# The gate of a fused attention and feed-forward kernel as one over one plus an exponential

## The chip, the cores and the metric

The kernel runs on one core of one Trainium2 chip. The metric is the time of one execution on the device in microseconds (us). Over three runs the kernel before the change took 1265.78, 1266.6 and 1267.1 us; the median is 1266.6 us.

The engines are named as the profile names them. PE is the matrix engine, and PEld its loading of weights. DVE is the vector engine, ACT the scalar engine (activation functions and copies), POOL the third elementwise engine, and SP the queue that issues the DMAs. Each engine works through its own instructions in order and waits on semaphores for the others.

## What is computed

The first half is attention of 512 local and 32 global tokens for 8 batches and 8 heads of width 64. Its output is the input `x` of a gated feed-forward layer of 4608 tokens, 512 channels and 1536 hidden channels. The change touches only the gate:

```python
def _moe_ref(x, w_gate, w_val, w_out) -> np.ndarray:
    gate = 1.0 / (1.0 + np.exp(-(x @ w_gate)))
    val = x @ w_val
    return (gate * val @ w_out).astype(np.float32)
```

## The kernel before

Matmuls run on float32r operands. Each operand is split into a high and a low part, and three of the four products are summed, so a product of two matrices costs three matmuls per block. The high part is a copy on ACT, the low part a subtraction on POOL.

`ffn_stream` walks through 120 **items**. An item is one chunk of tokens with one of the 12 blocks of 128 hidden channels. The first 24 items belong to two half chunks of 256 tokens and alternate between them; the next 84 belong to seven chunks of 512 tokens; the last 12 to one chunk of 256 global tokens. For an item PE issues 12 matmuls into a PSUM bank `bank_g` (the gate), 12 into `bank_v` (the value), and then the matmuls into `bank_o` that belong to the item before it. Between `bank_g` and `bank_o` the other engines do the following (tile names in the profile's manner):

- ACT L370: `th` = tanh of half of `bank_g`
- DVE L375: `mn` = the smaller of `bank_g` and 0, then ACT L376: `mn` = its exponential. For every second of the first 24 items ACT L372 and L373 do this in place of DVE and ACT.
- ACT L377: `th` = its absolute value
- DVE L378: `th` = (`th` + 1) times `mn`, which is twice the gate
- DVE L380: `th` = `bank_v` times `th`
- ACT L382 and POOL L383: the high and low parts `hh`, which are the operand of the `bank_o` matmuls

The factor 2 is taken out when the finished `bank_o` is copied to `ob` (L402 on ACT, L404 on DVE).

Attention of the next chunk runs between the groups of these matmuls, and so up to the last chunk but one of 512 tokens. Its units (two blocks of 128 queries of a head, or the global queries of a head) are generators with four stages that a queue of events starts at fixed ticks of the feed-forward. A unit's way over the engines is: scores on PE (L225), masked and reduced on DVE (L237), exponential on ACT (L240), reciprocal of the row sums on DVE (L243, L244), normalising mostly on DVE (L213, `p_buf`), transposition on PE (L254), high part on ACT (L263) and low part on DVE (L264, `pt`), product with the values on PE (L280, L281), and the sum of its parts (ACT L283, DVE L284, POOL L285). The global unit has the same steps in L299 to L337. The first chunks' attention runs without the splits, and the first 24 items also share DVE, ACT and POOL with the conversion of the weights (L128 to L138).

The python order of these calls is the starting point; a scheduler then arranges the instructions of each engine, so the order on an engine isn't the order of the lines. `bank_g`, `bank_v` and the attention's `bank_x` and `bank_y` share four PSUM banks in turn (tag "att"), and a bank is free again only when DVE or ACT has read it. `th` and `mn` have one buffer each.

Of the kernel before, what the change touches and what calls it, by code (L numbers as in the profile page):

```python
# [8 lines left out]
F32 = mybir.dt.float32  # L9
F32R = mybir.dt.float32r  # L10
U32 = mybir.dt.uint32
AF = mybir.ActivationFunctionType
ALU = mybir.AluOpType
# [4 lines left out]
P = 128  # L18
# [11 lines left out]
WIN = 224  # L30
DM = 512

# Where work is issued, in ticks of the feed-forward (one tick is four 512-token
# matmuls). Attention units of a chunk follow each other every PER ticks; a unit's
# stages lie STAGES apart, its operands are loaded and split ahead of it.
BASE, PER = 3, 4
STAGES = (0, 3, 6, 9)
LOAD_QK, LOAD_V, SPLIT_QK, SPLIT_V = 16, 9, 10, 4
LOAD_V_NATIVE = 4
# from the first of these ticks of a chunk on, attention is put off by the second  # L40
HOLE = (8, 1)
START = dict(per0=4, base1=1, per1=1.1, base2=23, per2=3, x2=28, lead=8, native_heads=4)
CONVERT = (-2, 4, 1, 3)
CONVERT_EARLY = (-985, -980, -977)
# the engines that share a kind of operation in turn: v(ector), s(calar)
NORM = {0: "v", 1: "v", 2: "ssv", 3: "sv"}
REBASE = "vs"

# [1 line left out]
NF = DF // P  # L50
KT = DM // P
# [3 lines left out]
def kernel(ctx, tc, qk, v, w_gate, w_val, w_out, out_l, out_g):  # L55
    nc = tc.nc
# [10 lines left out]
    ffn = ctx.enter_context(tc.tile_pool(name="ffn", bufs=1))  # L67
    dram = ctx.enter_context(tc.tile_pool(name="dram", bufs=1, space=DRAM))
    ps = ctx.enter_context(tc.tile_pool(name="ps", bufs=1, space=PSUM))

# [1 line left out]
    ident = const.tile([P, P], F32, name="ident")  # L72
    make_identity(nc, ident)
    NEG = -8.0e9
    masks = const.tile([P, 3, WIN], F32, name="masks")
    nc.gpsimd.memset(masks[:, 1], 0.0)
    # window column c < 96 stands for key c - 32, c >= 128 for key c - 64
    # (relative to the block's first query); the columns between are global
    mid = masks[:, 1]
    for c0, lo, hi in ((0, 0, 64), (128, 96, -32)):  # L80
        cols = mid[:, c0:c0 + 96]
# [13 lines left out]
    nc.vector.memset(pg, 0.0)  # L95
    xg32 = const.tile([P, KT, NG], F32, name="xg32")

# [1 line left out]
    wg = [const.tile([P, KT, DF], F32R, name=f"wg{i}") for i in range(2)]  # L99
    wv = [const.tile([P, KT, DF], F32R, name=f"wv{i}") for i in range(2)]  # L100
    wo_dram = [dram.tile([P, 2, DM], F32, name=f"wo_dram{f}") for f in range(NF)]
# [15 lines left out]
            nc.sync.dma_start(st, src)  # L117

    def convert(i, hi, lo):
        """The two float32r parts of a float64 [128, KT or 1, n] block, given as words."""  # L120
        src = w_src[i]
        t, n = src.shape[1], src.shape[2] // 2
        st, v = (o[i % len(o)].rearrange("p (t n) -> p t n", t=t) for o in conv_bufs)
        words = st.rearrange("p t (n two) -> p t n two", two=2)
        low, high = words[:, :, :, 0], words[:, :, :, 1]
        vf, hf = v.bitcast(F32), high.bitcast(F32)
        with tc.issue_after(anchor[0].ins) if i < 3 else nullcontext():
            nc.vector.tensor_scalar(v, high, 0x80000000, None, op0=ALU.bitwise_and)  # L128
            # read as a float32, the high word times 2^-112 has its exponent rebased to
            # float32's, with zeros between the sign and the exponent's eight bits  # L130
            if REBASE[i % len(REBASE)] == "s":
                nc.scalar.mul(hf, hf, 2.0 ** -112)
            else:
                nc.vector.tensor_scalar(hf, hf, 2.0 ** -112, None, op0=ALU.mult)
            nc.vector.scalar_tensor_tensor(v, low, 29, v, op0=ALU.logical_shift_right, op1=ALU.bitwise_or)
            nc.vector.scalar_tensor_tensor(v, high, 3, v, op0=ALU.logical_shift_left, op1=ALU.bitwise_or)
        nc.scalar.copy(hi, vf)
        nc.gpsimd.tensor_tensor(lo, vf, hi.bitcast(F32), op=ALU.subtract)  # L138
        stage(i + len(conv_bufs[0]))
# [9 lines left out]
        nc.sync.dma_start(wo_dram[f][:, 0], hi[:, 0].bitcast(F32))  # L149
        nc.sync.dma_start(wo_dram[f][:, 1], lo[:, 0].bitcast(F32))  # L150

# [1 line left out]
    def qcol(j):  # L153
        return j * P if j < 2 else Q1 + (j - 2) * P

# [180 lines left out]
        nc.vector.tensor_tensor(y, o_ps[0:64], y, op=ALU.add)  # L336
        nc.gpsimd.tensor_tensor(xg, y[:, 0:32], y[:, 32:64], op=ALU.add)  # L337

# [1 line left out]
    hl_q = []  # L340

    def x_split(xt, x32, kt, x0, ntok):
# [2 lines left out]
        nc.gpsimd.tensor_tensor(xt[:, 1, kt, xs], x32[:, 0:ntok], xt[:, 0, kt, xs].bitcast(F32), op=ALU.subtract)  # L345

    def ffn_stream(items):
        """Items (chunk, block of the hidden dimension); yields the part of a full
        512-token step that was issued, between groups of matmuls."""
        prev = None  # L350
        wo = None
        for n_it in range(len(items) + 1):
            if n_it < len(items):
                C, f = items[n_it]
                ntok, x0, xt = C["ntok"], C["x0"], C["xt"]()
                fs = slice(f * P, (f + 1) * P)
                for w, nm in ((wg, "bank_g"), (wv, "bank_v")):
                    acc = ps.tile([P, 512], F32, name=nm, tag="att", bufs=4)[:, 0:ntok]
                    n = 0
                    for a, c in ((0, 0), (1, 0), (0, 1)):  # L360
                        for t in range(KT):
                            nc.tensor.matmul(acc, w[a][:, t, fs], xt[:, c, t, x0:x0 + ntok],  # L362
                                             start=n == 0, stop=n == 11)
                            n += 1
                        if n < 12:
                            yield ntok / 512
                    if nm == "bank_g":
                        th = ffn.tile([P, 512], F32, name="th", bufs=1)[:, 0:ntok]
                        mn = ffn.tile([P, 512], F32, name="mn", bufs=1)[:, 0:ntok]
                        nc.scalar.activation(th, acc, AF.Tanh, scale=0.5)  # L370
                        if n_it < 2 * NF and n_it % 2:
                            nc.scalar.activation(mn, acc, AF.Relu, scale=-1.0)  # L372
                            nc.scalar.activation(mn, mn, AF.Exp, scale=-1.0)  # L373
                        else:
                            nc.vector.tensor_scalar(mn, acc, 0.0, None, op0=ALU.min)  # L375
                            nc.scalar.activation(mn, mn, AF.Exp)  # L376
                        nc.scalar.activation(th, th, AF.Abs)  # L377
                        nc.vector.scalar_tensor_tensor(th, th, 1.0, mn, op0=ALU.add, op1=ALU.mult)  # L378
                    else:
                        nc.vector.tensor_tensor(th, acc, th, op=ALU.mult)  # L380
                        hh = ffn.tile([P, 2, 512], F32R, name="hh", bufs=2)
                        nc.scalar.copy(hh[:, 0, 0:ntok], th)  # L382
                        nc.gpsimd.tensor_tensor(hh[:, 1, 0:ntok], th, hh[:, 0, 0:ntok].bitcast(F32), op=ALU.subtract)  # L383
                    yield ntok / 512
                if not (wo is not None and items[n_it - 1][1] == f):
                    wo = ffn.tile([P, 2, DM], F32R, name="wo", bufs=2)
                    nc.sync.dma_start(wo.bitcast(F32), wo_dram[f])
            if prev is not None:
                C2, f2, ph, pwo = prev
                nt = C2["ntok"] // P  # L390
                if f2 == 0:
                    C2["o"] = [ps.tile([P, DM], F32, name=f"bank_o{C2['o0'] + t}") for t in range(nt)]
                o_ps = C2["o"]
                for i, (a, c) in enumerate(((0, 0), (1, 0), (0, 1))):
                    for t in range(nt):
                        nc.tensor.matmul(o_ps[t], ph[:, a, t * P:(t + 1) * P], pwo[:, c],  # L396
                                         start=f2 == 0 and i == 0, stop=f2 == NF - 1 and i == 2)
                    if f2 == NF - 1 and i == 2:
                        for t in range(nt):
                            ob = ffn.tile([P, DM], F32, name="ob", bufs=2)  # L400
                            if t % 2:
                                nc.scalar.mul(ob, o_ps[t], 0.5)  # L402
                            else:
                                nc.vector.tensor_scalar(ob, o_ps[t], 0.5, None, op0=ALU.mult)  # L404
                            nc.sync.dma_start(C2["dst"][t * P:(t + 1) * P, :], ob)
                    yield nt / 4
            prev = (C, f, hh, wo) if n_it < len(items) else None

    # ---- driver: attention of the next chunk runs between the matmul groups
    def att_events(ci, start, per, tail=0):  # L410
        """(tick, order, thunk) of all attention work for chunk ci."""
        b, blocks, with_g = chunks[ci]
        ntok = len(blocks) * P
        x0 = (blocks[0] * P) % 512
# [40 lines left out]
    chunks = [(0, [0, 1], False), (0, [2, 3], True)] + [(b, [0, 1, 2, 3], True) for b in range(1, NB)]  # L455
    xts = {0: xp.tile([P, 2, KT, 512], F32R, name="xt")}
    xts[1] = xts[0]
    words = xp.tile([P, 4096], U32, name="xt")
# [7 lines left out]
                        xt=lambda ci=ci: xts[ci], dst=out_l[r0:r0 + len(blocks) * P, :]))  # L466
    G = len(chunks)
    chs.append(dict(ntok=NG, x0=0, o0=0, first=False, xt=lambda: xts[G], dst=out_g))
    # the first two half chunks share the steps in which the weights are converted
    lead = START["lead"]  # L470
    items = [(chs[0], f) for f in range(lead)] + [(chs[1], f) for f in range(lead)]
    for f in range(lead, NF):
# [1 line left out]
    for c in chs[2:]:  # L474
        items += [(c, f) for f in range(NF)]

    # events on the feed-forward's clock: one tick is four 512-token matmuls
    queue = att_events(0, -1000, START["per0"]) + att_events(1, START["base1"], START["per1"])
    queue += att_events(2, START["base2"], START["per2"])
    for ci in range(3, G):  # L480
# [83 lines left out]
```

## Time and profile before

| | |
|---|---|
| median of three runs | 1266.6 us |
| span of the profiled execution | 1265.6 us |
| items 0 to 23 (256 tokens, with attention and conversion of weights) | 50 to 272 us |
| items 24 to 95 (512 tokens, with attention) | 272 to 1105 us, 139 us for each chunk of 12 |
| items 96 to 107 (512 tokens, no attention) | 1105 to 1206 us |
| items 108 to 119 (256 global tokens) and the end | 1206 to 1265 us |

The stages are read from the times at which the `bank_g` matmuls of the items start. All times and durations are those of one profiled execution. A group row of the profile reads: line, engine, operation, written tile and read tile, shapes, count; then the group's busy time and the mean duration in ns of one; then how long the engine had been idle just before these instructions, and what ended that idleness. A row of stretches gives, for each stretch of time, every engine's busy time with its number of instructions, the granted clock of PE, and the share and rate of the DMA.

### The profile page before, as it was taken

How to read it: one execution, taken by the hardware profiler on the slowest of the kernel's cores; microseconds unless marked ns; L12 is line 12 of the kernel's file. 1: busy time of each engine (PE TensorE's matmuls, PEld its weight loads, DVE VectorE, ACT ScalarE, POOL GpSimd, SP SyncE). 2: the span in 40 equal slices, each digit the busy share in tenths (PEclk: the TensorE clock that was granted, in tenths of full speed). 3: DMA queues.
4: the chain of work that ended last, by engine and by line, in shares of the span. 5: the costliest groups of instructions: out<-in, count | busy, mean ns of one | idle time of the engine just before them, and what ended most of it. 6: DMA issues, size and time to landing. Idle time of an engine off the chain costs nothing.

```text
span 1265.6 us, 20474 instructions
## 1 busy us (share of the span) xinstructions
PE 1221.5 (97%) x6820; PEld 994.1 (79%) x6820; DVE 877.6 (69%) x2433; ACT 783.3 (62%) x1899; POOL 570.6 (45%) x573
## 2 busy tenths in 40 slices
PE   5899989999999999999999999999999999999998
PEld 4676768788788877888788877888788877888897
DVE  4797976757877777857876778767775787632232
ACT  4586766756666666666666667756765766532233
POOL 1444554545555355545555455535554555311111
PEclk9698999999999999999999999999999999999999
DMA  5576864333333333333333423343334332122143
GB/s 198 197 259 225 254 191 145 92 121 99 92 107 98 115 99 108 91 121 108 107 92 107 126 78 107 109 127 111 92 86 126 116 92 87 44 90 67 67 133 117
DMA packets 59497, 151.90 MB, mean 120 GB/s; under 512 B 6144, under 2 KB 19456, under 8 KB 59392
## 3 DMA queue, kind: packets, MB, share of 16 engines
q1 hardware_dynamic: 59392, 150.59, 38.9%
q8 instruction: 54, 0.88, 0.3%
q14 instruction: 51, 0.42, 0.1%
HBM read 135.36 MB, written 15.20 MB: 119 GB/s over the span
## 4 chain that ended last, share of the span: by engine, by line
PE 77%; DVE 13%; ACT 5%; issue 3%; POOL 1%; DMA 1%; SPq 0%; POOLq 0%; DVEq 0%; ACTq 0%
PE bank_g L362 20%; PE bank_v L362 19%; PE bank_o L396 19%; PE bank_x L225 5%; PE bank_y L254 4%; DVE p_buf L213 3%; DVE th L378 2%; PE bank_y L317 2%; PE bank_x L330 2%; PE bank_x L280 2%; PE bank_x L299 2%; PE bank_x L281 1%; DVE pg_buf L213 1%; ACT s_sb L240 1%; DVE pt L264 1%
## 5 line engine op out<-in xcount | busy, mean ns | idle before, releaser
L362 PE MATMUL bank_g<-xt,wg 128*128 128x512 f32 (+1 forms) x1440 | 340.3, 371 | 1.8 <-DVE th L380 1.8
L362 PE MATMUL bank_v<-xt,wv 128*128 128x512 f32 (+1 forms) x1440 | 332.6, 368 | 3.0 <-DVE pt L264 2.7
L396 PE MATMUL bank_o<-wo,hh 128*128 128x512 f32 x1224 | 334.0, 404 | 0.8 <-ACT hh L382 0.4
L362 PEld LDWEIGHTS bank_g<-xt,wg 128*128 128x128 f32 x1440 | 238.6, 192 | 41.6 <-issue 3.4
L362 PEld LDWEIGHTS bank_v<-xt,wv 128*128 128x128 f32 x1440 | 237.8, 190 | 40.7 <-PE bank_y L301 3.1
L396 PEld LDWEIGHTS bank_o<-wo,hh 128*128 128x128 f32 x1224 | 214.1, 189 | 38.9 <-ACT hh L382 1.2
L383 POOL TENSOR_TENSOR hh<-th,hh 128x512 fp32r<-128x512 f32 (+1 forms) x120 | 137.6, 1147 | 199.7 <-ACT hh L382 198.8
L240 ACT ACTIVATE s_sb<-s_sb,nm 128x224 f32<-128x224 f32 x240 | 113.8, 475 | 143.1 <-DVE nm L237 142.0
L213 DVE TENSOR_SCALAR p_buf<-s_sb,r 128x128 f32<-128x128 f32 (+1 forms) x443 | 151.8, 386 | 4.2 <-PE bank_y L254 0.4
L375 DVE TENSOR_SCALAR mn<-bank_g 128x512 f32<-128x512 f32 (+1 forms) x108 | 67.3, 623 | 110.7 <-ACT th L370 109.3
L378 DVE SCALAR_TENSOR_TENSOR th<-th,mn 128x512 f32<-128x512 f32 (+1 forms) x120 | 101.5, 846 | 59.0 <-ACT mn L376 52.7
L285 POOL TENSOR_TENSOR x<-t 64x256 f32<-64x256 f32 x104 | 76.4, 734 | 142.8 <-DVE t L284 138.7
L194 POOL TENSOR_TENSOR kl<-qk_raw,qk_hi 128x704 fp32r<-128x704 f32 x52 | 88.4, 1701 | 114.8 <-ACT qk_hi L193 114.8
L370 ACT ACTIVATE th<-bank_g 128x512 f32<-128x512 f32 (+1 forms) x120 | 63.5, 529 | 97.7 <-PE bank_g L362 96.1
L382 ACT CAST hh<-th 128x512 fp32r<-128x512 f32 (+1 forms) x120 | 66.5, 554 | 68.1 <-DVE th L380 67.3
L237 DVE CUSTOM_DVE_ANT_0 s_sb<-bank_x,masks 128x224 f32<-128x224 f32 x240 | 83.8, 381 | 12.7 <-PE bank_x L225 8.4
L254 PE MATMUL bank_y<-ident,p_buf 128*128 128x128 f32 x496 | 80.1, 282 | 10.8 <-DVE p_buf L213 6.6
L196 POOL TENSOR_TENSOR qk_hi<-qk_raw,qk_hi 64x256 fp32r<-64x256 f32 x104 | 87.7, 863 | 4.1
L254 PEld LDWEIGHTS bank_y<-ident,p_buf 128*128 128x128 f32 x496 | 60.9, 143 | 32.5 <-ACT pg_buf L308 6.6
L243 DVE TENSOR_SCALAR r<-sm 128x2 f32<-128x2 f32 x128 | 29.3, 229 | 75.5 <-ACT s_sb L240 74.2
L193 ACT CAST qk_hi<-qk_raw 128x1248 fp32r<-128x1248 f32 x52 | 64.1, 1233 | 22.2 <-PE bank_y L301 22.1
L380 DVE TENSOR_TENSOR th<-bank_v,th 128x512 f32<-128x512 f32 (+1 forms) x120 | 72.4, 604 | 5.1 <-PE bank_v L362 1.3
(109 smaller groups left out, 1985.9 us busy)
## 6 DMA issues: line engine op xcount, KB each, us to landing
wo<-wo_dram SPq DMA_DIRECT2D x116, 512.0 KB, 3.5
qk_raw<-in_qk_dram SPq DMA_DIRECT2D x104, 312.0 KB, 4.4
v_raw<-in_v_dram SPq DMA_DIRECT2D x52, 256.0 KB, 2.6
out_dram<-ob SPq DMA_DIRECT2D x34, 256.0 KB, 3.0
xt<-in_w_gate_dram SPq DMA_DIRECT2D x12, 512.0 KB, 4.5
xt<-in_w_val_dram SPq DMA_DIRECT2D x12, 512.0 KB, 4.4
xt<-in_w_out_dram SPq DMA_DIRECT2D x12, 512.0 KB, 4.9
v_nat<-in_v_dram SPq DMA_DIRECT2D x8, 512.0 KB, 5.5
```

What stands on the lines that cost most here:

```text
L194: nc.gpsimd.tensor_tensor(kl, t[:, K0:Q1], hi[:, K0:Q1].bitcast(F32), op=ALU.subtract)
L196: nc.gpsimd.tensor_tensor(hi[64:128, r], t[64:128, r], hi[64:128, r].bitcast(F32), op=ALU.subtract)
L213: nc.vector.tensor_scalar(out, in_, by, None, op0=ALU.mult)
L237: anchor[0] = nc.vector.tensor_tensor_reduce(out=s_sb[:, i], in0=s_ps[:, i, 0:WIN], in1=masks[:, m], scale=-0.125, scalar=3.0e38, op0=ALU. ...
L240: nc.scalar.activation(s_sb[:, i], s_sb[:, i], AF.Exp, bias=nm[:, i:i + 1], scale=-1.0, accum_out=sm[:, i:i + 1])
L254: nc.tensor.transpose(pt_ps[:, 2 * i + t], pb[:, i, t * P:(t + 1) * P], ident)
L285: nc.gpsimd.tensor_tensor(dst, t0[:, :, 0], t0[:, :, 1], op=ALU.add)
L362: nc.tensor.matmul(acc, w[a][:, t, fs], xt[:, c, t, x0:x0 + ntok], start=n == 0, stop=n == 11)
L378: nc.vector.scalar_tensor_tensor(th, th, 1.0, mn, op0=ALU.add, op1=ALU.mult)
L380: nc.vector.tensor_tensor(th, acc, th, op=ALU.mult)
L383: nc.gpsimd.tensor_tensor(hh[:, 1, 0:ntok], th, hh[:, 0, 0:ntok].bitcast(F32), op=ALU.subtract)
L396: nc.tensor.matmul(o_ps[t], ph[:, a, t * P:(t + 1) * P], pwo[:, c], start=f2 == 0 and i == 0, stop=f2 == NF - 1 and i == 2)
```

## The change

The gate is computed as the reciprocal of one plus the exponential of the negated `bank_g`. Three instructions take the place of the five (or, for every second of the first 24 items, six): the exponential on ACT reads the bank, a two-operation instruction on DVE adds 1 and limits the sum to 1e38, and DVE's reciprocal follows, both in place in `th`. The tile `mn` is gone from the loop. Since the result is the gate itself, the copies of `bank_o` lose their factor of one half. Comments of the file were removed as well.

```diff
                     if nm == "bank_g":
                         th = ffn.tile([P, 512], F32, name="th", bufs=1)[:, 0:ntok]
-                        mn = ffn.tile([P, 512], F32, name="mn", bufs=1)[:, 0:ntok]
-                        nc.scalar.activation(th, acc, AF.Tanh, scale=0.5)
-                        if n_it < 2 * NF and n_it % 2:
-                            nc.scalar.activation(mn, acc, AF.Relu, scale=-1.0)
-                            nc.scalar.activation(mn, mn, AF.Exp, scale=-1.0)
-                        else:
-                            nc.vector.tensor_scalar(mn, acc, 0.0, None, op0=ALU.min)
-                            nc.scalar.activation(mn, mn, AF.Exp)
-                        nc.scalar.activation(th, th, AF.Abs)
-                        nc.vector.scalar_tensor_tensor(th, th, 1.0, mn, op0=ALU.add, op1=ALU.mult)
+
+                        nc.scalar.activation(th, acc, AF.Exp, scale=-1.0)
+                        nc.vector.tensor_scalar(th, th, 1.0, 1.0e38, op0=ALU.add, op1=ALU.min)
+                        nc.vector.reciprocal(th, th)
                     else:
                         nc.vector.tensor_tensor(th, acc, th, op=ALU.mult)
...
                             if t % 2:
-                                nc.scalar.mul(ob, o_ps[t], 0.5)
+                                nc.scalar.copy(ob, o_ps[t])
                             else:
-                                nc.vector.tensor_scalar(ob, o_ps[t], 0.5, None, op0=ALU.mult)
+                                nc.vector.tensor_copy(ob, o_ps[t])
```

In the changed kernel the exponential is line 370, the addition line 371, the reciprocal line 372, the product with `bank_v` line 374, the high part line 376 and the low part line 377.

The scheduler arranges the engines anew around these instructions. On DVE, in the third item of the second chunk of 512 tokens (around the 39th product with `bank_v`), stands before:

```order
L213 TENSOR_SCALAR p_buf<-s_sb,r 128x128
L375 TENSOR_SCALAR mn<-bank_g 128x512
L324 TENSOR_TENSOR ptg<-bank_y,ptg 128x5x32
L213 TENSOR_SCALAR p_buf<-s_sb,r 128x96
L378 SCALAR_TENSOR_TENSOR th<-th,mn 128x512
L237 ISA s_sb,nm<-bank_x,masks 128x224
```

At the same item of the changed kernel stands on DVE:

```order
L213 TENSOR_SCALAR p_buf<-s_sb,r 128x128
L371 TENSOR_SCALAR th<-th 128x512
L324 TENSOR_TENSOR ptg<-bank_y,ptg 128x5x32
L372 RECIPROCAL th<-th 128x512
L213 TENSOR_SCALAR p_buf<-s_sb,r 128x96
L374 TENSOR_TENSOR th<-bank_v,th 128x512
L237 ISA s_sb,nm<-bank_x,masks 128x224
```

The reciprocal stands where the merging step stood, one place earlier: the last normalising of `p_buf`, on which the transposition on PE waits, and the next unit's scores (L237) are now behind it. The product with `bank_v` has moved ahead of those scores.

On ACT, three items later (the 42nd of the instructions that read `bank_g`), stands before:

```order
L370 ACTIVATE th<-bank_g 128x512
L335 COPY y<-bank_x 64x64
L377 ACTIVATE th<-th 128x512
L205 CAST vhl<-v_raw 128x8x64
L376 ACTIVATE mn<-mn 128x512
L263 CAST pt<-bank_y 128x512
L193 CAST qk_hi<-qk_raw 128x1248
```

and in the changed kernel:

```order
L370 ACTIVATE th<-bank_g 128x512
L335 COPY y<-bank_x 64x64
L205 CAST vhl<-v_raw 128x8x64
L263 CAST pt<-bank_y 128x512
L193 CAST qk_hi<-qk_raw 128x1248
```

The absolute value and the exponential of `mn` are gone there, and the attention's copies have closed up behind the one pass over `bank_g` that is left.

## The prediction

> **What bounds the kernel now.** I read the page's busy line first, then the chain of work that ended last, then the stretches of time by stage.
>
> ```profile
> span 1265.6 us, 20474 instructions
> PE 1221.5 (97%) x6820; PEld 994.1 (79%) x6820; DVE 877.6 (69%) x2433; ACT 783.3 (62%) x1899; POOL 570.6 (45%) x573
> PE 77%; DVE 13%; ACT 5%; issue 3%; POOL 1%; DMA 1%; SPq 0%; POOLq 0%; DVEq 0%; ACTq 0%
> ```
>
> PE is busy for 97% of the span and carries 77% of the chain. Next stands DVE. The stretches show how near it is in each stage; each row has PE, PEld, DVE, ACT, POOL in this order.
>
> ```profile
> 50.00:272.00 222.00, 208.12 (x1382) 168.69 (x1383) 177.92 (x488) 156.53 (x452) 110.00 (x100) 0.96 0.60 188
> 410.00:549.00 139.00, 137.67 (x753) 112.07 (x752) 104.41 (x294) 92.35 (x214) 71.59 (x73) 1.00 0.36 106
> 1105.00:1206.00 101.00, 101.00 (x439) 81.51 (x438) 26.43 (x39) 31.60 (x52) 18.98 (x17) 1.00 0.22 73
> 1206.00:1265.00 59.00, 54.79 (x374) 50.02 (x372) 17.39 (x39) 21.18 (x51) 9.26 (x13) 0.99 0.41 134
> ```
>
> In a steady chunk (second row, one of six alike) 12 items take 139 us: 139 / 12 = 11.58 us for an item, with PE idle for only 1.3 us in all. DVE works 104.41 / 12 = 8.70 us for an item, so it has 2.9 us to spare. In the last 24 items, without attention, DVE has 70% and more to spare.
>
> **What goes.** These are groups of the six steady chunks (272 to 1105 us, 72 items).
>
> ```profile
> L375 DVE TENSOR_SCALAR mn<-bank_g 128x512 f32<-128x512 f32 x72 | 49.0, 680 | 20.2 <-ACT th L370 18.7
> L378 DVE SCALAR_TENSOR_TENSOR th<-th,mn 128x512 f32<-128x512 f32 x72 | 72.4, 1006 | 36.2 <-ACT mn L376 36.2
> L377 ACT ACTIVATE th<-th 128x512 f32<-128x512 f32 x72 | 45.8, 636 | 1.3
> L376 ACT ACTIVATE mn<-mn 128x512 f32<-128x512 f32 x72 | 45.4, 631 | 16.6 <-DVE mn L375 14.5
> ```
>
> DVE loses 0.68 + 1.01 = 1.69 us per item, which leaves 7.01. ACT loses 0.64 + 0.63 = 1.27 us of its 92.35 / 12 = 7.70. ACT is not the bound, so this is worth nothing by itself. The tanh turns into an exponential over the same bank and costs the same. The copies of `bank_o` lose a factor and keep their shape: nothing.
>
> **What comes: the addition.** One instruction on DVE with two constants, from SBUF to SBUF. Its nearest rows are an f32 multiplication of the weights' conversion (over the whole trace) and the widest normalisation (steady chunks).
>
> ```profile
> L134 DVE TENSOR_SCALAR xt<-xt 128x512 f32<-128x512 f32 x18 | 9.0, 498 | 0.1
> L213 DVE TENSOR_SCALAR pg_buf<-pg_buf,mg 32x576 f32<-32x576 f32 x48 | 44.4, 925 | 1.7
> ```
>
> Between 0.50 and 0.93 us; I take 0.60, near the row with the same shape, and 0.40 for the 256-token items.
>
> **What comes: the reciprocal.** This decides everything, and the trace has it only on one and on two elements per partition.
>
> ```profile
> L244 DVE RECIPROCAL r<-r x128: 143/166/177, 13.0 to 1091.8; 128x2 f32<-128x2 f32 x128
> L312 DVE RECIPROCAL mg<-mg x64: 140/151/153, 61.1 to 1097.2; 32x1 f32<-32x1 f32 x64
> L304 DVE TENSOR_REDUCE mg<-bank_x 32x1 f32<-32x512 f32 x48 | 32.2, 671 | 2.4 <-PE bank_y L301 2.4
> L305 DVE TENSOR_REDUCE mg<-bank_y 32x1 f32<-32x32 f32 x48 | 8.1, 169 | 0.0
> ```
>
> The three numbers of the first two rows are minimum, median and maximum in ns. An ordinary DVE instruction costs (671 - 169) / 480 = 1.05 ns per further element, by the two reductions. From one element to two the reciprocal's median grows by 15 ns, its minimum by 3 ns. That is a thin basis, for two instructions only, with other neighbours, but even 3 ns is well above 1.05. The ends are therefore 1.05 ns, which gives 0.151 + 511 x 0.00105 = 0.69 us for 512 elements, and 15 ns, which gives 7.8 us. I take the middle, 8 ns: 0.151 + 511 x 0.008 = **4.24 us**, and 0.151 + 255 x 0.008 = 2.19 us for 256.
>
> [...]
>
> **The sum, steady chunks.** DVE's work per item becomes 7.01 + 0.60 + 4.24 = 11.85 us, already over the 11.58 that PE needs. DVE also keeps waits that the gate has nothing to do with: in each attention unit it waits for the exponential's row sums.
>
> ```profile
> L243 DVE TENSOR_SCALAR r<-sm 128x2 f32<-128x2 f32 x96 | 22.1, 230 | 67.8 <-ACT s_sb L240 67.8
> L311 DVE TENSOR_SCALAR mg<-sg 32x1 f32<-32x1 f32 x48 | 9.6, 200 | 39.7 <-ACT pg_buf L309 39.7
> ```
>
> (67.8 + 39.7) / 72 = 1.49 us per item of idleness before L243 and L311. The order of the changed kernel keeps L243 close behind the L237 pair it depends on, so I keep all of it: 13.34 us per item, 1.76 more than 11.58. For 72 items: **+127 us**. PE, which was the bound, will wait for `p_buf`, for `pt` and for free banks, all queued behind a reciprocal. In these terms the point at which DVE overtakes PE lies at a reciprocal of 11.58 - 7.01 - 0.60 - 1.49 = 2.48 us, or 4.6 ns per element.
>
> **The sum, items 0 to 23.** All rows are of 50 to 272 us.
>
> ```profile
> L375 DVE TENSOR_SCALAR mn<-bank_g 128x256 f32<-128x256 f32 x12 | 4.9, 408 | 2.7 <-ACT th L370 2.7
> L378 DVE SCALAR_TENSOR_TENSOR th<-th,mn 128x256 f32<-128x256 f32 x24 | 15.7, 655 | 7.7 <-ACT mn L373 2.7 <-POOL kl L194 2.6 <-ACT mn L376 1.4
> L243 DVE TENSOR_SCALAR r<-sm 128x2 f32<-128x2 f32 x24 | 5.9, 246 | 6.3 <-ACT s_sb L240 6.3
> L311 DVE TENSOR_SCALAR mg<-sg 32x1 f32<-32x1 f32 x16 | 3.2, 198 | 7.5 <-ACT pg_buf L309 7.5
> ```
>
> DVE works 177.9 of 222 us. Without 4.9 + 15.7 = 20.6, and with 24 x (0.40 + 2.19) = 62.2, it works 219.5; with the kept waits of 6.3 + 7.5 it needs 233.3 us, so **+11 us**.
>
> **The sum, items 96 to 119.** A 512-token item takes 101 / 12 = 8.4 us here, and DVE's part becomes about 26.43 / 12 - 1.38 + 4.84 = 5.7 (L375 and L378 cost 0.69 each here): hidden behind PE, as `hh` is needed only after the next item's 24 matmuls. Only the last item's chain is bare.
>
> ```profile
> 1256.15 0.38 ACT L370 ACTIVATE th<-bank_g 128x256 f32<-128x256 f32 x1 [1.48 <-PE bank_g L362]
> 1257.54 0.42 DVE L378 SCALAR_TENSOR_TENSOR th<-th,mn 128x256 f32<-128x256 f32 x1 [0.55 <-ACT mn L376]
> 1258.07 0.42 DVE L380 TENSOR_TENSOR th<-bank_v,th 128x256 f32<-128x256 f32 x1
> ```
>
> From the bank's reading to the product passed 1.92 us; afterwards 0.38 + 0.40 + 2.19 and about 0.1 of handing over, 3.1: **+1 us**.
>
> Together 1265.6 + 127 + 11 + 1 = 1404.6 for the profiled execution. The median of the runs lies 1.0 above its span, so **1406 us**.
>
> **The rivals.**
>
> *Not slower: the reciprocal runs like any other DVE instruction.* At 0.69 us the two new instructions cost 1.29 per item where 1.69 went, and ACT has 1.27 us less. For it speaks the minimum's small growth of 3 ns; against it the medians. It decides as soon as the reciprocal is under about 2.5 us. PE would gain part of what it waits for DVE now.
>
> ```profile
> PE bank_y L254 <- DVE p_buf L213: 6.6, 5, 2.7
> PE bank_x L280 <- DVE pt L264: 6.5, 13, 1.0
> PE bank_v L362 <- DVE pt L264: 2.7, 6, 0.5
> PE bank_y L317 <- DVE pg_buf L213: 2.2, 9, 0.6
> ```
>
> These rows (all waits of the trace by total) sum to 18 us; half of that and a little of the start gives 10 us: 1256 us. [...]
>
> *The cover holds.* The reciprocal costs 4.24 us, but the kept waits are filled by the new order. Then a steady item takes DVE's 11.85 us: 72 x 0.27 = 19, and 1286 us with the rest. Against it: DVE works strictly in order, and what stands between L237 and L243 is little.
>
> *The long reciprocal.* At 15 ns per element an item takes 16.9 us, and the 24 first ones 1.79 us more each than in my sum: 1265.6 + 384 + 54 + 3, about 1707 us.
>
> **How the numbers follow.** The forecast, DVE as the bound with 1300 to 1500 us, has a chance of 0.60; 1500 is a reciprocal of some 5.4 us (10 ns per element). More than that 0.06. The cover holds, or nearly so, to 1270 to 1300: 0.07. The reciprocal close to the point of balance, no change: 0.05. The ordinary reciprocal: 0.22. Slower by over 0.2% is thus 0.73, within 0.2% (about what a measurement of this kernel can tell) 0.05, faster 0.22. For eight in ten the range has to reach into the last case: 1256 to 1500 us. The likeliest case's own range is 1300 to 1500.
>
> **What would show it.** The row of L372 at 128x512: about 4200 ns for the forecast, under 2500 for either faster rival. In a steady chunk DVE should be busy for about 142 us of a chunk of about 160, with PE at 138 as before, and PE's waits should name DVE `pt`, `p_buf` and `th`; the waits before L243 should still come to about 1.5 us per item with the ones before L311. Stretches after the last attention should be as long as before. Wrong would be the price of one element first of all, then the assumption that DVE's own waits stay, and then that nothing else on DVE changes its duration.

## The result and the profile after

The changed kernel takes 1385.85 us (median of four runs, 1383.04 to 1386.99) where the kernel before takes 1266.55: 1.0926 times as long, 95% interval 1.0897 to 1.0954. The profiled execution has a span of 1383.4 us, 117.8 more than before. The prediction was 1406 us.

Busy times and the chain of work that ended last, from the page of the changed kernel:

```profile
span 1383.4 us, 20144 instructions
PE 1261.2 (91%) x6820; PEld 1010.7 (73%) x6820; DVE 1103.8 (80%) x2445; ACT 652.0 (47%) x1647; POOL 567.6 (41%) x573
PE 45%; DVE 38%; ACT 10%; issue 4%; POOL 2%; DMA 0%; SPq 0%; DVEq 0%; ACTq 0%; POOLq 0%
PE bank_v L362 12%; DVE th L372 11%; PE bank_o L390 11%; PE bank_g L362 10%; DVE p_buf L213 8%; ACT s_sb L240 6%; PE bank_x L225 3%; PE bank_y L254 2%; DVE pt L264 2%; DVE t L284 2%; DVE th L374 2%; DVE s_sb L237 2%; DVE r L243 2%; DVE th L371 2%; PE bank_x L280 1%
```

PE's share of the chain fell from 77% to 45%, DVE's rose from 13% to 38%, and the reciprocal alone (L372) carries 11%. ACT was relieved by 131 us (783.3 to 652.0), and this shows nowhere in the time.

The stretches (length, then PE, PEld, DVE, ACT, POOL): the first row is the last 60 items with attention of the kernel before, the other three are of the changed kernel in this order: its items 0 to 23, the same 60 items, and the 512-token items without attention. They come from two traces, so there are two fences.

```profile
410.00:1106.00 696.00, 689.17 (x3762) 561.40 (x3762) 522.22 (x1470) 459.65 (x1071) 351.60 (x356) 1.00 0.35 102
```

```profile
49.00:299.00 250.00, 218.98 (x1381) 176.66 (x1381) 203.16 (x498) 137.76 (x392) 112.30 (x100) 0.91 0.52 167
454.00:1221.00 767.00, 712.02 (x3759) 567.14 (x3758) 652.34 (x1470) 385.46 (x950) 347.90 (x356) 0.99 0.31 93
1221.00:1322.00 101.00, 101.00 (x439) 81.57 (x439) 54.96 (x39) 17.33 (x30) 17.74 (x15) 1.00 0.21 73
```

An item of these 60 went from 696 / 60 = 11.60 us to 767 / 60 = 12.78. DVE now works 652.34 / 60 = 10.87 us of it, in place of 8.70, and is idle for 1.91. By the starts of the `bank_g` matmuls, items 24 to 95 take 88 us more (833.5 to 921.7), items 0 to 23 28.5 more (222.4 to 250.9), the last 24 nothing more; the end takes 2 us more and the beginning 1 less. PE's own busy time in the 60 items grew as well, from 689.17 to 712.02 us for practically the same number of instructions, at a granted clock of 0.99 in place of 1.00. So 48 of the 71 us are PE's waiting; what lengthened the rest is not shown. DVE's share in the stage without attention doubled, from 26.43 to 54.96 us of 101, and costs nothing there, since PE is busy for all of it.

What DVE does in the 60 items (groups by line; L243, L311, L371 and L264 with what ended the idleness before them):

```profile
L372 DVE RECIPROCAL th<-th 128x512 f32<-128x512 f32 x60 | 200.7, 3345 | 0.9
L213 DVE TENSOR_SCALAR p_buf<-s_sb,r 128x128 f32<-128x128 f32 x160 | 89.0, 557 | 3.0
L264 DVE TENSOR_TENSOR pt<-bank_y,pt 128x512 fp32r<-128x512 f32 x80 | 54.0, 675 | 9.2 <-ACT pt L263 8.9
L371 DVE TENSOR_SCALAR th<-th 128x512 f32<-128x512 f32 x60 | 32.7, 545 | 15.8 <-ACT th L370 15.2
L243 DVE TENSOR_SCALAR r<-sm 128x2 f32<-128x2 f32 x80 | 20.7, 259 | 55.8 <-ACT s_sb L240 55.8
L311 DVE TENSOR_SCALAR mg<-sg 32x1 f32<-32x1 f32 x40 | 8.0, 199 | 12.9 <-ACT pg_buf L309 12.9
```

The reciprocal takes 3.35 us. The waits before L243 stayed at 55.8 / 60 = 0.93 us per item; the four rows of waits come to (9.2 + 15.8 + 55.8 + 12.9) / 60 = 1.56 of the 1.91 us. And PE, in the same stretch, waits for what stands behind the reciprocal on DVE:

```profile
PE bank_v L362 <- DVE pt L264: 16.1, 10, 2.4
PE bank_x L280 <- DVE pt L264: 15.8, 35, 1.6
PE bank_y L254 <- DVE th L374: 15.7, 13, 1.7
PE bank_y L254 <- DVE p_buf L213: 7.1, 15, 0.5
```

The first and the third are waits for a bank: `bank_v` cannot start before DVE has read a `bank_y`, and a `bank_y` not before the product has read a `bank_v`.

### The profile page after: what moved, and what is told of

It reads as the page before. It is cut to its first block, busy times and chain, and to the rows that moved or that the text cites. A ratio compares the mean times of both kernels' runs of the same rounds, so it can differ in the third digit from the quotient of the medians.

```text
span 1383.4 us, 20144 instructions
## 1 busy us (share of the span) xinstructions
PE 1261.2 (91%) x6820; PEld 1010.7 (73%) x6820; DVE 1103.8 (80%) x2445; ACT 652.0 (47%) x1647; POOL 567.6 (41%) x573
## 4 chain that ended last, share of the span: by engine, by line
PE 45%; DVE 38%; ACT 10%; issue 4%; POOL 2%; DMA 0%; SPq 0%; DVEq 0%; ACTq 0%; POOLq 0%
PE bank_v L362 12%; DVE th L372 11%; PE bank_o L390 11%; PE bank_g L362 10%; DVE p_buf L213 8%; ACT s_sb L240 6%; PE bank_x L225 3%; PE bank_y L254 2%; DVE pt L264 2%; DVE t L284 2%; DVE th L374 2%; DVE s_sb L237 2%; DVE r L243 2%; DVE th L371 2%; PE bank_x L280 1%
## 5 line engine op out<-in xcount | busy, mean ns | idle before, releaser
L362 PE MATMUL bank_v<-xt,wv 128*128 128x512 f32 (+1 forms) x1440 | 341.8, 376 | 19.8 <-DVE pt L264 19.3
L390 PE MATMUL bank_o<-wo,hh 128*128 128x512 f32 x1224 | 336.6, 407 | 10.9 <-POOL hh L377 6.4
L372 DVE RECIPROCAL th<-th 128x512 f32<-128x512 f32 (+1 forms) x120 | 343.9, 2866 | 2.0
L362 PEld LDWEIGHTS bank_v<-xt,wv 128*128 128x128 f32 x1440 | 245.0, 196 | 60.2 <-issue 22.2
L390 PEld LDWEIGHTS bank_o<-wo,hh 128*128 128x128 f32 x1224 | 221.1, 192 | 54.3 <-POOL hh L377 8.7
L213 DVE TENSOR_SCALAR p_buf<-s_sb,r 128x128 f32<-128x128 f32 (+1 forms) x443 | 169.1, 427 | 4.4 <-PE bank_y L254 0.6
L371 DVE TENSOR_SCALAR th<-th 128x512 f32<-128x512 f32 (+1 forms) x120 | 58.1, 484 | 95.1 <-ACT th L370 94.4
L254 PE MATMUL bank_y<-ident,p_buf 128*128 128x128 f32 x496 | 85.4, 286 | 40.0 <-DVE th L374 18.8
L283 ACT COPY t<-bank_x 64x512 f32<-64x512 f32 x104 | 60.8, 584 | 100.5 <-PE bank_x L281 99.4
L237 DVE CUSTOM_DVE_ANT_0 s_sb<-bank_x,masks 128x224 f32<-128x224 f32 x240 | 82.8, 378 | 16.0 <-PE bank_x L225 9.8
L370 ACT ACTIVATE th<-bank_g 128x512 f32<-128x512 f32 (+1 forms) x120 | 63.7, 531 | 63.8 <-PE bank_g L362 47.1
L243 DVE TENSOR_SCALAR r<-sm 128x2 f32<-128x2 f32 x128 | 32.4, 253 | 74.6 <-ACT s_sb L240 73.1
L206 POOL TENSOR_TENSOR vhl<-v_raw,vhl 128x512 fp32r<-128x512 f32 x52 | 67.2, 1293 | 57.5 <-ACT vhl L205 56.0
L196 POOL TENSOR_TENSOR qk_hi<-qk_raw,qk_hi 64x256 fp32r<-64x256 f32 x104 | 78.2, 772 | 8.1 <-issue 4.1
```

The source lines that it names most:

```text
L196: nc.gpsimd.tensor_tensor(hi[64:128, r], t[64:128, r], hi[64:128, r].bitcast(F32), op=ALU.subtract)
L213: nc.vector.tensor_scalar(out, in_, by, None, op0=ALU.mult)
L237: anchor[0] = nc.vector.tensor_tensor_reduce(out=s_sb[:, i], in0=s_ps[:, i, 0:WIN], in1=masks[:, m], scale=-0.125, scalar=3.0e38, op0=ALU. ...
L254: nc.tensor.transpose(pt_ps[:, 2 * i + t], pb[:, i, t * P:(t + 1) * P], ident)
L371: nc.vector.tensor_scalar(th, th, 1.0, 1.0e38, op0=ALU.add, op1=ALU.min)
L372: nc.vector.reciprocal(th, th)
```

## The experiments

Theory 1 is the prediction's: the reciprocal's length on DVE is the cause, and an item of the steady chunks takes what DVE works and what it waits for ACT. The rivals are named in each expectation. "Item" means the mean of items 36 to 95, the 60 shown above.

### The reciprocal replaced by a multiplication

```diff
-                        nc.vector.reciprocal(th, th)
+                        nc.vector.tensor_scalar(th, th, 0.5, None, op0=ALU.mult)
```

> The changed kernel with a multiplication by one half in place of the reciprocal, same shape and place on DVE (so the gate is not computed). Theory 1 (DVE is the bound: its work plus its own waits for ACT, 10.90 + 1.88 = 12.78 us for an item of the steady chunks against PE's 11.58; the reciprocal of 3.35 us is the cause): DVE falls to about 8.0 + 1.5 us, PE is the bound again and the time is 1256 to 1268 us. Rival A (the new order of the instructions or the addition costs a good part of the 119 us): 1290 us or more. The 256-token items of the start give back their 28 us under theory 1.

Measured: 1255.78 us, 0.9901 times the kernel before (0.9872 to 0.993), at the lower edge of what theory 1 expected. Its 60 items:

```profile
407.00:1094.00 687.00, 686.31 (x3764) 563.14 (x3762) 489.70 (x1470) 388.00 (x950) 353.20 (x356) 1.00 0.35 103
```

11.45 us per item, with PE busy for 686 of 687. Items 0 to 23 took 224.1 us in place of 250.9. So the whole loss of 119 us hangs on this one instruction, and 11 us of gain come with the rest of the change. It is the prediction's first rival, priced there at 1256 us: that is what the change would have given with a reciprocal at the price of this multiplication.

### The reciprocal in four pieces between other work

```diff
-                        nc.vector.reciprocal(th, th)
+                        nc.vector.reciprocal(th[:, 0 * ntok // 4:(0 + 1) * ntok // 4], th[:, 0 * ntok // 4:(0 + 1) * ntok // 4])
...
                         if n < 12:
                             yield ntok / 512
+                        if nm == "bank_v":
+                            k = n // 4
+                            q = slice(k * ntok // 4, (k + 1) * ntok // 4)
+                            nc.vector.reciprocal(th[:, q], th[:, q])
```

> The reciprocal in four pieces of a quarter of the columns, one behind the first group of matmuls of the gate's item and the others behind the groups of the value matmuls, so that other work of DVE stands between them. By 6.25 ns per element (3346 ns for 512, 1745 for 256) a piece of 128 costs about 0.95 us, four of them 3.8, 0.43 more than the one; of 64 columns 0.55, 2.2 in place of 1.75. Theory 1 (the sum of DVE's work and its waits): slower than the changed kernel, by 72 x 0.43 + 24 x 0.44 = 41 us, about 1425 us. Rival B (it is the length of the one block that holds up pt, p_buf and the banks behind it): faster than the changed kernel, 1310 to 1360 us, as the others pass between the pieces.

Measured: 1382.49 us, 1.0895 (1.0857 to 1.0932), the same as the changed kernel within the intervals. Neither expectation was met. The stretch of the 60 items, and the pieces in it:

```profile
453.00:1221.00 768.00, 711.75 (x3762) 573.89 (x3761) 644.96 (x1650) 386.31 (x951) 347.10 (x356) 0.98 0.31 93
```

```profile
L370 DVE RECIPROCAL th<-th 128x128 f32<-128x128 f32 x180 | 159.3, 915 | 0.0
L213 DVE TENSOR_SCALAR p_buf<-s_sb,r 128x128 f32<-128x128 f32 x160 | 79.3, 495 | 1.4
L376 DVE RECIPROCAL th<-th 128x128 f32<-128x128 f32 x60 | 56.9, 949 | 0.9
```

In the shown stretch the four pieces cost (159.3 + 56.9) / 60 = 3.60 us in place of 3.35, but other instructions of DVE became shorter, the normalisations of 128 columns most (495 in place of 557 ns), and DVE works 10.75 us and not more; the item takes 12.80. Rival B's gain did not come: the same work in these pieces takes the same time. Two of the four pieces mostly stood side by side, so a finer interleaving was not tried, and a cost of the block's length is not excluded by this run alone.

### One more half reciprocal, which nothing reads

```diff
                         nc.vector.reciprocal(th, th)
+                        spare = ffn.tile([P, 512], F32, name="spare", tag="mn", bufs=1)[:, 0:ntok // 2]
+                        nc.vector.reciprocal(spare, th[:, 0:ntok // 2])
```

> The changed kernel with one more reciprocal, of half of the gate's columns into a tile that nothing reads. It adds 1.75 us to each 512-token item and about 0.95 to each 256-token item on DVE. Theory 1: every microsecond shows in the steady chunks and at the start: 72 x 1.75 + 24 x 0.95 = 149 us, about 1535 us; nothing in the last 24 items. Rival C (what hurts is the gate's own chain, reciprocal to product to freeing bank_v, and not DVE's load): clearly less than that, below 1470 us, since nothing waits for the extra result.

Measured: 1510.37 us (one run; its granted clock in the 60 items is 0.96, in place of 0.99). The 60 items:

```profile
472.00:1323.00 851.00, 747.88 (x3758) 580.76 (x3757) 751.37 (x1530) 383.35 (x950) 345.51 (x357) 0.96 0.28 83
```

14.18 us per item: 1.40 more than the changed kernel, for 12.52 - 10.87 = 1.65 us more of DVE's work. The cost shows nearly whole and the time lies above the 1470 us of rival C. Yet this does not settle rival C. Nothing reads the extra result, but in each of these items the extra reciprocal stands on DVE between the gate's reciprocal and the product, so the product comes later too. From the start of ACT's reading of `bank_g` (L370) to the end of the product pass 4.65 us on the mean of the 60 items with the multiplication, 6.67 in the changed kernel and 8.70 here. DVE's load and the gate's own chain grew together. Two parts of the expectation failed: items 0 to 23 took only 4.5 us more in place of 23, and the last 24 with the end, where nothing was expected, took 23 us more. In that last stage PE's longest wait is for the high part `hh` (8.3 us in all), which is the end of the gate's chain.

### The kernel before with an added reciprocal, of a half and of a quarter

```diff
                         nc.vector.scalar_tensor_tensor(th, th, 1.0, mn, op0=ALU.add, op1=ALU.mult)
+                        nc.vector.reciprocal(mn[:, 0:ntok // 2], th[:, 0:ntok // 2])
```

and the same with `ntok // 4`.

> The kernel before the change with a reciprocal of half of the columns added on DVE behind the merging step, into the tile mn that is dead there. DVE's steady item becomes 8.70 + 1.75 = 10.45 us of work; with its waits of 1.5 to 1.9 us it needs 11.9 to 12.3 against PE's 11.58. Theory 1: 72 x 0.35 to 0.75 = 25 to 54 us and some 23 us for the start (24 x 0.95): 1315 to 1345 us. Rival D (DVE's waits are filled by whatever work there is, so that only work over 11.58 us counts): no change in the steady chunks, 1290 us at most.

> The kernel before the change with a reciprocal of a quarter of the columns added on DVE behind the merging step, into the dead tile mn: 0.95 us for a 512-token item and about 0.55 for a 256-token item. Theory 1, with the idleness that the runs so far left to DVE (1.7 to 2.3 us for a steady item): 8.70 + 0.95 + 2.0 = 11.6 us, just at PE's 11.58, so at most 10 us in the steady chunks, and 24 x 0.55 = 13 us at the start: 1270 to 1292 us. Rival E (any added DVE time on the way to the product costs its full length, without a point of balance): 72 x 0.95 + 13 = 81, about 1348 us.

Measured: with the half 1352.33 us, 1.0661 (1.0611 to 1.0711); with the quarter 1298.32 us, 1.024 (1.0219 to 1.0261). The 60 items of the half, then of the quarter:

```profile
443.00:1187.00 744.00, 705.09 (x3768) 560.05 (x3767) 608.35 (x1530) 455.86 (x1071) 352.32 (x356) 1.00 0.33 96
```

```profile
419.00:1133.00 714.00, 696.71 (x3762) 560.72 (x3762) 565.49 (x1530) 457.87 (x1070) 353.87 (x357) 1.00 0.34 100
```

Items of 12.40 and 11.90 us. DVE works 10.14 and 9.42 us and is idle for 2.26 and 2.48. A reciprocal costs in the old kernel too, so neither the new order nor the new instructions of the gate are needed for the loss. The added one stands ahead of the product here too (from L370 to the product's end pass 5.09 us before the change, 6.01 with the quarter and 6.72 with the half), so these two runs do not separate DVE's load from the gate's chain either. But both came out slower than theory 1 allowed (1315 to 1345, and 1270 to 1292): the point of balance is not sharp. With the quarter, 0.72 us more of DVE's work costs 0.30 us per item although by theory 1 it should just have fitted. Rivals D and E, as they were stated, both fall.

### The normalisation moved to ACT, and its control

```diff
-NORM = {0: "v", 1: "v", 2: "ssv", 3: "sv"}
+NORM = {0: "s", 1: "v", 2: "ssv", 3: "sv"}
```

> The changed kernel with the normalisation of the attention of all later chunks moved from DVE to ACT; the reciprocal of the gate stays whole. DVE's steady item loses the normalising, (89.0 + 46.8 + 24.3) / 60 = 2.7 us: 8.2 us of work and 10.1 with its idleness, under PE's 11.58; ACT grows from 6.4 to about 9 us. Theory 1 (DVE's whole load is what decides, and the 3.35 us block by itself does no harm): steady items back to 11.45 to 11.7 us, only the start keeps its loss: 1265 to 1300 us. Rival B (the one block of 3.35 us holds up pt and the banks, whatever else DVE has to do): above 1340 us. Rival F (ACT, now the carrier of the normalising between its other work, becomes the next wait): steady items of 12 us or more.

Measured: 1329.47 us, 1.0495 (1.0471 to 1.0518), outside theory 1. The 60 items and DVE's own waits in them:

```profile
429.00:1164.00 735.00, 700.21 (x3762) 559.83 (x3762) 521.44 (x1110) 498.20 (x1310) 343.83 (x356) 1.00 0.33 97
```

```profile
DVE pt L264 <- ACT pt L263: 58.6, 65, 1.4
DVE r L243 <- ACT s_sb L240: 43.4, 55, 1.0
DVE mg L311 <- ACT pg_buf L309: 26.6, 30, 1.6
DVE s_sb L237 <- ACT p_buf L211: 23.8, 15, 2.1
```

DVE has as little work as in the kernel before (8.69 us) and ACT 8.30, yet the item takes 12.25 us, as rival F forecast; DVE is idle for 3.56, mostly waiting for ACT (2.54 us by the four rows). Is it ACT's new work, then? The control has the multiplication in place of the gate's reciprocal, everything else equal:

> The control for the kernel with the normalisation on ACT: the same, with a multiplication by one half in place of the gate's reciprocal (so the gate is not computed). That kernel took 12.25 us for a steady item although DVE worked only 8.69 of them and ACT 8.29. Rival F (the normalisation on ACT is itself the loss): 12.0 us or more here too, 1300 us and up. Rival B (the reciprocal still costs, by its length, although DVE has room): 11.45 to 11.65 us as without attention on ACT, 1252 to 1272 us.

Measured: 1251.56 us, 0.9861 (0.9829 to 0.9893), items of 686 / 60 = 11.43 us:

```profile
406.00:1092.00 686.00, 685.28 (x3762) 564.28 (x3761) 364.28 (x1111) 501.70 (x1311) 344.29 (x356) 1.00 0.36 104
```

So ACT's new work by itself costs nothing, and rival F falls. It is the reciprocal again that costs 0.82 us per item, in a kernel where DVE is idle for 3.56 us. Here too the gate's chain from L370 to the product's end is longer, 5.98 us against 4.49 in the control. Two trials for the reason followed: the reciprocal in four pieces in this kernel, and the last stage of the attention issued later.

> The kernel with the normalisation on ACT and the reciprocal in four pieces with other work between them. DVE has 3.56 us of room in an item there, so the 0.34 us that the pieces cost more don't count. Rival B (the length of the one block decides where DVE has room): steady items of 11.8 us or less, 1300 us or less. Rival F (ACT's place in the attention's way decides): no gain, 1320 to 1340 us.

Measured: 1330.42 us, 1.0483 (1.045 to 1.0516). Items of 726 / 60 = 12.10 us in place of 12.25, given back in items 0 to 23 (244 us in place of 236). Rival B's gain does not come here either.

### The attention's last stage later

```diff
-STAGES = (0, 3, 6, 9)
+STAGES = (0, 3, 6, 9.9)
```

> The kernel with the normalisation on ACT and the whole reciprocal, and the attention's last stage (the product with the values, which waits for pt) issued one group of four matmuls later (9.9 ticks in place of 9). Theory 2 (where DVE has room, the loss is that the orders of PE, ACT and DVE were made for a short gate, and PE comes to pt too early behind a reciprocal of 3.35 us): PE's waits for pt, some 0.45 us per steady item, shrink and the item falls from 12.25 to 11.6 to 11.9 us: 1275 to 1305 us. Rival G (DVE and ACT lose the time in waits for each other, wherever PE's matmul stands): 12.1 us or more, 1320 us or more.

> The changed kernel with the attention's last stage issued one group of four matmuls later (9.9 ticks in place of 9). Theory 1 (DVE's work of 10.87 us and the 1.7 to 2.3 us that it always stays idle make the item): 12.6 us or more, 1365 to 1390 us, whatever PE's place. Theory 2 (PE comes to pt too early): PE's waits for pt of 0.53 us per item go and the item falls to 12.3 us or less, 1350 us or less.

Measured: with the normalisation on ACT 1326.31 us, 1.0445 (1.04 to 1.049), items of 734 / 60 = 12.23 us, as without the shift and as rival G forecast. For the changed kernel itself 1367.38 us, 1.079 (1.073 to 1.0851); its 60 items, and what PE waits for in them:

```profile
458.00:1215.00 757.00, 705.88 (x3760) 570.87 (x3759) 639.01 (x1470) 386.67 (x950) 349.83 (x356) 0.99 0.32 94
```

```profile
PE bank_x L330 <- DVE ptg L324: 18.8, 20, 1.7
PE bank_x L280 <- DVE pt L264: 9.9, 15, 0.9
PE bank_v L362 <- DVE pt L264: 9.0, 10, 1.1
```

PE's waits for `pt` fell from 31.9 to 18.9 us, and a new one for `ptg` (18.8) came in their place. The item takes 12.62 us with DVE at 10.65 and idle for 1.97, about the same idleness as before the shift. The profiled execution was the slowest of four (1378.78 us), so this item lies on the long side. Theory 2, that PE merely comes too early, gets neither of its two forecasts, and theory 1 has both of its own here: where PE stands changes what it waits for more than how long. It is not without effect, though: the median is 18 us below that of the changed kernel, and the intervals of the two ratios do not overlap.

### A gate without a reciprocal

The change's gain without its cost: half of one plus the hyperbolic tangent (the "tangent" of the expectation) of half the argument. The addition goes into the product, the half stays in the last copies. By the formula small gates lose relative digits in that sum, which the kernel before avoids with its merging step; no run here measures how many.

```diff
                         th = ffn.tile([P, 512], F32, name="th", bufs=1)[:, 0:ntok]
-                        mn = ffn.tile([P, 512], F32, name="mn", bufs=1)[:, 0:ntok]
                         nc.scalar.activation(th, acc, AF.Tanh, scale=0.5)
...
-                        nc.scalar.activation(th, th, AF.Abs)
-                        nc.vector.scalar_tensor_tensor(th, th, 1.0, mn, op0=ALU.add, op1=ALU.mult)
                     else:
-                        nc.vector.tensor_tensor(th, acc, th, op=ALU.mult)
+                        nc.vector.scalar_tensor_tensor(th, th, 1.0, acc, op0=ALU.add, op1=ALU.mult)
```

> The gate as half of one plus the tangent of half the argument: one ACT instruction, and the addition of 1 goes into the product with the value, so neither a reciprocal nor an instruction of its own is left on DVE for it. The factor one half stays in the last copies. DVE's steady item is 8.70 - 1.69 = 7.0 us, ACT's 7.70 - 1.27 = 6.4. Theory 1: PE is the bound in the steady chunks at 11.45 us, as with the cheap stand-in; 1248 to 1258 us.

Measured: 1259.21 us, 0.9935 (0.9912 to 0.9958), just above the range that was expected. Together with the normalisation on ACT:

> The gate as half of one plus the hyperbolic tangent of half the argument (one ACT instruction, the addition inside the product with the value), and the attention's normalisation on ACT. DVE then works about 5 us of a steady item, ACT 8.3. PE is the bound in the steady chunks at 11.43 us as in the control with the cheap stand-in, and the start, which took 216.7 us there in place of 224, gains a little: 1247 to 1256 us. If instead only the steady chunks matter, as with the normalisation on DVE: 1255 to 1263 us.

Measured: 1241.6 us, **0.9806** (0.978 to 0.9832), the fastest of all; whether the gain reaches 2% is open. Its 60 items:

```profile
397.00:1080.00 683.00, 683.00 (x3764) 565.13 (x3764) 308.88 (x990) 501.88 (x1311) 342.80 (x356) 1.00 0.36 104
```

PE is busy for all of the 683 us (11.38 per item) and DVE works only 5.15. Items 0 to 23 took 214.6 us in place of 222.4. The 1241.6 us lie below both ranges that were expected. Of the 12.1 us between the spans of this run and of the control with the multiplication (1238.7 and 1250.8), 6.0 lie ahead of the first item, 2.1 in items 0 to 23 and 3.8 in items 24 to 95; why the first item starts earlier is not shown.

## Why the prediction was right, and where it was off

- **DVE takes the path from PE: right.** The replacement by a multiplication gives all 119 us back and 11 more. The chain and PE's waits name `pt`, `p_buf` and the product, as forecast. PE's busy time did not stay at 138 us for a chunk, as was put: it is 712.02 / 5 = 142.4. That DVE's load as such sets the time is not shown (the last point).
- **The price of the reciprocal: too high.** The middle of 1.05 and 15 ns gave 8 ns per element and 4.24 us; the row of 512 elements shown above and the one of 256 (in items 0 to 23 of the changed kernel) give (3345 - 1741) / 256 = 6.27 ns, and 3.35 us for 512.

```profile
L372 DVE RECIPROCAL th<-th 128x256 f32<-128x256 f32 x23 | 40.0, 1741 | 0.1
```

- **DVE's work: right by its terms.** 7.01 + 0.55 + 3.35 = 10.9 us against 10.87 measured; the addition took 0.545 us where 0.60 was put. That the rest came out unchanged is a balance of two shifts: the 128-wide normalisations grew from 459 to 557 ns each, and the global ones (`pg_buf`) shrank from 913 to 606. The exponential over `bank_g` cost what the tanh had cost, a median of 597 ns in both traces (L370), and the copies of `bank_o` without their factor took 587 ns on ACT and 685 on DVE in place of 598 and 692 (medians), so both could be left out of the sum.
- **The waits that stay: the right rows, too small a sum.** 1.49 us were kept and 1.91 are there. The wait before L243 stayed as it was, the one before L311 shrank from 0.55 to 0.21 us, and waits before L371 and L264 (0.42 us together) came in, for which the sum had no term. The one before L371 could have been kept: it is the wait for ACT's reading of `bank_g`, which the prediction's own row of L375 shows (20.2 / 72 = 0.28 us before, 15.8 / 60 = 0.26 after).
- **Items 0 to 23: too small.** 11 us were put, 28.5 came, although the reciprocal was shorter. The sum kept 13.8 us of DVE's waits; with 203.16 of 250 us busy DVE is idle for 46.8. The run with the multiplication shows that the loss is the reciprocal's. PE is idle for 31 us there, in place of 14, and its longest wait is for the gate's own result:

```profile
PE bank_o L390 <- POOL hh L377: 6.4, 3, 2.5
PE bank_o L390 <- ACT hh L376: 2.2, 3, 1.0
```

  The sum had no term for that.
- **The last 24 items: right**, nothing but 2 us at the end, where 1 was put.
- **Taken together two errors offset each other, and that the sum came within some 20 us is luck.** With the measured 3.35 and 0.55 us the sum's own steps give items of 12.39 us, 58 us for 72 of them and about 1 for the start: some 1326 us for the profiled execution. The too high price added some 79 us; the waits and the start, which the sum did not have, were worth some 57.
- **The point of balance: wrong as a sharp line.** It was put at a reciprocal of 2.48 us. In the kernel before, an added 0.95 us already costs 0.30 per item. And with the normalisation on ACT, DVE at 8.69 us of work still gives 12.25 per item. DVE's work plus two microseconds describes the runs in which DVE does the normalising and PE is not busy throughout (idleness 1.7 to 2.5 us), but it is not a law of the kernel: with the normalisation on ACT the two engines wait for each other, with neither full (ACT works 8.30 us of the 12.25, and waits 58.3 us in all for DVE's L237 between 464 and 1150 us). Pieces in place of the block did not change this, and PE's matmuls at another place changed little. Two explanations are left. One is that the orders of the three engines were arranged for a gate of ordinary length and lock into each other when it is longer; an order made for the real length was not tried. The other is the gate's own chain to the product, which frees `bank_v`: from L370 to the product's end it took 5.98 to 8.70 us in the five runs with a reciprocal at the gate for which it is given above, and 4.49 to 5.09 in the three without, though the time does not follow it strictly (6.67 us in an item of 12.78 us, 6.72 in one of 12.40). A reciprocal placed behind the product, which loads DVE and leaves that chain alone, was not tried. The way from the reciprocal to the loss stays open.

## What to carry to other kernels

Count passes by their price, not by their number: this change replaced five instructions by three and lost 9%, because one of the three costs 6.27 ns per element where the product behind it costs (678 - 411) / 256 = 1.04 (L374, 678 ns for 512 elements in the 60 items and 411 for 256 in items 0 to 23). An instruction known only on one or two elements should be measured once at full width before a design rests on it. And room on an engine is not room on its way: here an engine with 2.9 us of idleness in an item of 11.6 could not take 0.95 us for nothing; (57.2 + 32.7 + 30.2 + 15.8 + 14.3 + 1.3) / 60 = 2.5 us of that idleness were waits for ACT's answer (before L243, L311, L378, L375, L336 and L284). In the run with the added quarter DVE's work grew by 0.72 us and its idleness shrank by only 0.42.

## What was not expected of the hardware

The reciprocal's duration grows evenly (949 ns for 128 elements, 1741 for 256, 3345 for 512), which leaves about 0.14 us fixed; by that, one and two elements should differ by 6 ns, and the medians of the small ones differ by 15. So the difference of two short instructions was no measure of the slope. It also hardly varies: the 84 of 512 elements took 3330 to 3355 ns. The addition ahead of it, of the same shape and also within SBUF, took 404 to 1675 ns. The trace shows where the long ones lie: the 55 additions of 512 elements beside which POOL had no instruction running took 404 to 430 ns, and all longer ones are among the 29 with one beside them; the reciprocal's range is practically the same with and without (3330 to 3354 and 3331 to 3355 ns). The rows of the whole trace, with both widths:

```profile
L372 DVE RECIPROCAL th<-th x120: 1723/3337/3355, 54.6 to 1373.9; 128x512 f32<-128x512 f32 x84, 128x256 f32<-128x256 f32 x36
L371 DVE TENSOR_SCALAR th<-th x120: 260/409/1675, 54.0 to 1373.5; 128x512 f32<-128x512 f32 x84, 128x256 f32<-128x256 f32 x36
```
